# A conditional jump at the end of TensorE's and VectorE's programs, announced by a branch hint

## The chip, the cores and the metric

The kernel runs on one core of a Trainium2 chip. A core has five engines that each run a program of their own: TensorE (PE; its weight loads are listed apart as PEld), VectorE (DVE), ScalarE (ACT), GpSimd (POOL) and SyncE (SP). They meet through semaphores, and 16 DMA engines move data between the chip's memory and the core. The metric is the device time of one execution in microseconds (us), lower is better. It is compared as a median over runs; one execution is also recorded by the hardware profiler, and all views below are of that one.

## The reference, cut to what matters

One decode step: a layernorm, attention of one query token over the last 2048 positions of a key and value cache, and an MLP gate.

```
x  : 2 x 1 x 448            (B, S, D)     k_cache, v_cache : 2 x 8 x 8192 x 256
wq : 448 x 4096             wo : 4096 x 448       w1 : 448 x 1792      w2 : 1792 x 448

xn  = layernorm(x)
q   = (xn @ wq) as 16 heads of 256
s   = softmax(q k^T / 16) over the last 2048 positions; two query heads share one of 8 key heads
o   = (s v) put together to 2 x 4096, @ wo
g   = silu(relu(xn @ w1) @ w2)
out = x + o * g
```

All inputs and the output are bfloat16. Nearly all bytes are the two cache windows (16.8 MB each), the rest are the weights.

## The kernel before, in words

The kernel writes each engine's list of operations by hand. `_Prog` (line 23) holds five lists; `op` appends an operation, `dma` a transfer, each with the operations that it depends on. `run` (line 39) numbers the semaphores and then emits the lists one after the other: for every dependency that isn't known to be met it puts a wait (line 65) ahead of the operation. An engine works strictly in the order of its list. All of this is one straight block of code without a loop or a jump; an engine's program ends with its last operation.

The cache windows are taken as four units `u` (batch and half of the key heads) of 4 MB each, in four buffers `kv0` to `kv3`. SP issues all large loads in this order: wq, w1, w2, the four key units, then the value units into the same buffers as soon as the scores of that unit are done (`load_v`, the last unit in two halves), and last wo in six parts of 16, 4, 4, 4, 2 and 2 column tiles (`WO_PARTS`). Every one of these transfers is cut by rows over the 16 DMA engines, and its semaphore counts 16, one for each DMA engine, so that a part is there when the slowest of the 16 has brought its share.

The work goes in this order. VectorE and ScalarE do the layernorm and clear the banks. TensorE computes q (into `qbk`), then the MLP (`do_H`, `do_F`), VectorE makes the gate `g_sb`. For each key unit VectorE transposes the 4 MB buffer in four pieces (`do_turn`, line 276), TensorE makes the scores (`do_S`, into `sbk`), VectorE the maximum, ScalarE the exponentials (`do_max`), VectorE transposes them (`do_et`). `do_spread` puts all weights in place on TensorE, VectorE masks them (`do_pt`), then TensorE does the value products (`do_PV`, into `obk`) and VectorE scales them (`do_out`). At the end TensorE multiplies with wo, part by part as it lands (`direct`, into `fbk`; short unneeded products, `fill`, keep TensorE busy in between), and VectorE does the two last operations: the product with the gate (line 474) and the sum with x (line 476, `out_sb`). The output goes out in two halves, one issued by SP and one by ACT, and each of these two engines then waits for its own store:

```
        for c, eng in ((0, SP), (1, ACTE)):
            d_o = pr.dma(eng, out[:, 0, NCOL * c:NCOL * c + NCOL], out_sb[32 * c:32 * c + B, :], [v_o])
            pr.op(eng, None, [d_o])
```

TensorE, VectorE and GpSimd wait for no store.

Built, TensorE's program has 929 instructions of 64 bytes each, VectorE's 90, ScalarE's 27, SyncE's 24 and GpSimd's 20. An engine's instructions reach it by DMA too: the profile counts those packets as kind "instruction", on queues of their own.

Of the kernel before, what the change touches and what calls it, by code (L numbers as in the profile page):

```python
# [11 lines left out]
PE, DVE, ACTE, SP, POOL = "pe", "dve", "act", "sp", "pool"  # L12


class _Op:
    __slots__ = ("eng", "fn", "deps", "dma", "needed", "value", "sem")

    def __init__(self, eng, fn, deps, dma):
        self.eng, self.fn, self.deps, self.dma = eng, fn, deps, dma
        self.needed, self.value, self.sem = dma, 0, None  # L20


class _Prog:

    def __init__(self, nc, es):
        self.nc, self.es = nc, es
        self.lists = {PE: [], DVE: [], ACTE: [], SP: [], POOL: []}

    def op(self, eng, fn, deps=()):
# [9 lines left out]
    def run(self):  # L39
        nc = self.nc  # L40
        n = 0
        for ops in self.lists.values():
            for o in ops:
                for d in o.deps:
                    d.needed = True
        for e, ops in self.lists.items():
            sem, count = self.es.enter_context(nc.semaphore(f"s_{e}")), 0
            for o in ops:
                if o.dma:
                    n += 1  # L50
                    o.sem, o.value = self.es.enter_context(nc.semaphore(f"d_{n}")), 16
                elif o.needed:
                    count += 1
                    o.sem, o.value = sem, count

        def emit(eng, ops):
            seen = {}
            for o in ops:
                want = {}
                for d in o.deps:  # L60
                    if d.value > want.get(id(d.sem), (None, 0))[1]:
                        want[id(d.sem)] = (d.sem, d.value)
                for key, (sem, value) in want.items():
                    if value > seen.get(key, 0):
                        eng.wait_ge(sem, value)
                        seen[key] = value
                made = o.fn(eng) if o.fn else None
                if o.needed:
                    made.then_inc(o.sem, 16 if o.dma else 1)

        for eng, e in ((nc.sync, SP), (nc.gpsimd, POOL), (nc.scalar, ACTE), (nc.vector, DVE), (nc.tensor, PE)):
            emit(eng, self.lists[e])


def bass_recurrent_scan__sliding_block_cached__dense_activation_relu__decode_kernel(
# [11 lines left out]
    B, Sq, D = A_x.shape  # L87
# [14 lines left out]
    NCOL = D // 2  # L102
# [5 lines left out]
    with es:  # L108
        pr = _Prog(nc, es)

        def named(name, shape, dt):
            return es.enter_context(nc.sbuf_tensor(name, shape, dt))
# [4 lines left out]
        def view(t, off, dims, n=128, p0=0):  # L117
            width = t.shape[1]
            return bass.AP(t, p0 * width + off, [[width, n]] + dims)
# [28 lines left out]
        out_sb = named("out_sb", [128, NCOL], BF)  # L148
# [43 lines left out]
        for u in range(NU):  # L192
# [4 lines left out]
            out=ident[:, :], in_=ident[:, :], compare_op=ALU.not_equal, fill=1.0,  # L197
# [7 lines left out]
            out=sd[0:B, 0:1], in0=st2[0:B, 1:2], scalar1=EPS, scalar2=None, op0=ALU.add), [v_ag])  # L205
# [5 lines left out]
        def z(t):  # L211
            return a_z[t.name]
# [20 lines left out]
        for e2 in range(2):  # L233
            v_xn = pr.op(DVE, lambda e, e2=e2: e.tensor_scalar(  # L234
                out=view(xg, 128 - 127 * e2, [[256, 4], [128, 2], [2, 64]], n=B),
# [4 lines left out]
        def mm(out_ap, lhsT, rhs, start, stop=False, **kw):  # L240
            return lambda e: e.matmul(out_ap, lhsT=lhsT, rhs=rhs, start=start, stop=stop,  # L241
                                      skip_group_check=True, **kw)

        for s in range(SLOTS):
# [3 lines left out]
            out=view(xr, 0, [[4, SLOTS], [2, 2], [1, 2]]), in0=view(mbk, 0, [[2, SLOTS], [0, 2], [1, 2]]),  # L248
# [4 lines left out]
        for s in range(SLOTS):  # L253
# [6 lines left out]
            out=view(q_x, 0, [[256, 8], [128, 2], [1, 32]]), in0=view(qbk, 0, [[64, 8], [1, 2], [2, 32]]),  # L260
# [12 lines left out]
        def do_turn(u, lo, hi):  # L273
            kf = kv[u][:, :].bitcast(F32)
            for n in range(lo, hi):
                st["turn", u] = pr.op(DVE, lambda e, n=n: e.transpose(  # L276
                    kf[:, 2048 * n:2048 * n + 2048], kf[:, 2048 * n:2048 * n + 2048]), [d_k[u]])

        def do_S(u):
            b, hg = divmod(u, 2)  # L280
            deps = [st["turn", u], st["q"], z(sbk[u % 2]), st.get(("exp", u - 2))]
            for jp in range(8):
                j, par = divmod(jp, 2)
                for g in range(4):
                    o = pr.op(PE, mm(sbk[u % 2][32 * g:32 * g + 8, :],
                                     view(qstat, jp * 16 + 4 * g + 2 * hg + b, [[128, 8]]),
                                     view(kv[u], 64 * j + 2 * g + par, [[DH, NT], [8, 8]]),
                                     jp == 0, jp == 7, tile_position=(0, 32 * g)), deps)
                    deps = []
            last_S[u] = o  # L290
# [30 lines left out]
        def do_pt(u):  # L321
            st["pt", u] = pr.op(DVE, lambda e: e.tensor_tensor(  # L322
                out=view(pt[u], 0, [[8, 64], [2, 4], [1, 2]]), in0=view(spk, 128 * u, [[2, 64], [0, 4], [1, 2]]),
                in1=view(pmask, 0, [[0, 64], [1, 4], [0, 2]]), op=ALU.mult), [st["sp"], v_pm])
# [48 lines left out]
        def do_H():  # L373
            deps = [st["w1"], v_xr, v_q]
            for s in range(SLOTS):
                for k in range(4):
                    hf, i = divmod(k, 2)
                    lo = s * FC + i * 448
                    o = pr.op(PE, mm(qbk[32 * k:32 * k + B, 0:448], xr[:, 4 * s + 2 * hf:4 * s + 2 * hf + 2],
                                     w1_sb[:, lo:lo + 448], s == 0, s == SLOTS - 1, tile_position=(0, 32 * k)), deps)  # L380
                    deps = []
            v = pr.op(DVE, lambda e: e.tensor_scalar(
                out=h_n[:, :], in0=view(qbk, 0, [[1, 14], [14, 32]]),
                scalar1=0.0, scalar2=None, op0=ALU.max), [o])
            st["h"] = pr.op(DVE, lambda e: e.transpose(h_sb[:, :], h_n[:, :]), [v])

        def do_F():
            deps = [st["w2"], st["h"], z(fbk)]
            for j in range(14):
                i = j % 4  # L390
                o = pr.op(PE, mm(fbk[32 * i:32 * i + B, 0:D], h_sb[:, 32 * j:32 * j + 2], w2_sb[:, j * D:j * D + D],
                                 j < 4, j >= 10, tile_position=(0, 32 * i)), deps)
                deps = []
            v = pr.op(DVE, lambda e: e.tensor_copy(zc[:, :], fbk[:, 0:D]), [o])
            deps = [v, v_f8, st["mbk"]]
            for c in range(2):
                o = pr.op(PE, mm(mbk[32 * c:32 * c + B, 0:NCOL], f8[:, 0:B], zc[:, NCOL * c:NCOL * c + NCOL],
                                 True, True, tile_position=(0, 32 * c)), deps)
                deps = []
            a_e = pr.op(ACTE, lambda e: e.activation(ea[0:ROWS, :], mbk[0:ROWS, 0:NCOL], ACT.Exp, scale=-1.0), [o])  # L400
            v = pr.op(DVE, lambda e: e.tensor_scalar(
                out=ea[0:ROWS, :], in0=ea[0:ROWS, :], scalar1=1.0, scalar2=None, op0=ALU.add), [a_e])
            v = pr.op(DVE, lambda e: e.reciprocal(tmp[0:ROWS, :], ea[0:ROWS, :]), [v])
            st["g"] = st["mbk"] = pr.op(DVE, lambda e: e.tensor_tensor(
                out=g_sb[0:ROWS, :], in0=mbk[0:ROWS, 0:NCOL], in1=tmp[0:ROWS, :], op=ALU.mult), [v])
# [3 lines left out]

        do_H()  # L410
        do_F()
        do_turn(0, 0, 4)
        do_S(0)
        d_v[0] = load_v(0)
# [16 lines left out]
        do_rs()  # L431
        for u in range(1, NU):
            do_pt(u)
        for u in range(NU):
            do_PV(u)
            do_out(u)
            if u >= 2:
                do_turn_out(u - 2)
# [7 lines left out]
        for j in range(WO_TILED):  # L446
            i = j % 4
            o = pr.op(PE, mm(wbk[32 * i:32 * i + B, 0:D], at2[:, B * j:B * j + B], wqo[:, j * D:j * D + D],
                             j < 4, j >= WO_TILED - 4, tile_position=(0, 32 * i)), deps + [landed.get(j)])
# [19 lines left out]
        for j in range(20, 32):  # L469
# [5 lines left out]
            out=tmp[0:ROWS, :], in0=fbk[0:ROWS, 0:NCOL], in1=g_sb[0:ROWS, :], op=ALU.mult), [m_o, st["g"]])  # L475
        v_o = pr.op(DVE, lambda e: e.tensor_tensor(  # L476
            out=out_sb[0:ROWS, :], in0=tmp[0:ROWS, :], in1=x_c[0:ROWS, :], op=ALU.add), [v_t] + d_xc)
        for c, eng in ((0, SP), (1, ACTE)):
            d_o = pr.dma(eng, out[:, 0, NCOL * c:NCOL * c + NCOL], out_sb[32 * c:32 * c + B, :], [v_o])
            pr.op(eng, None, [d_o])  # L480

        pr.run()

# [27 lines left out]
```

## Time and profile before

| | |
|---|---|
| three runs | 110.45, 110.6 and 111.1 us; median 110.6 us |
| the profiled execution | 110.67 us |
| its span, from the first to the last instruction | 109.3 us |
| mean granted TensorE clock | 0.842 |
| busy: VectorE / TensorE / ScalarE / GpSimd | 62.2 / 57.0 / 9.1 / 2.1 us |
| DMA | 44.17 MB in 2616 packets, 404 GB/s over the span |
| last part of wo landed | 106.75 us |
| store issued; SP's wait for it over | 108.02 us; 109.3 us |

The span counts from the kernel's first instruction to its last. The time of the same execution is 1.32 us longer (110.67 less 109.35 in the trace's full figure); what lies in that difference isn't in the profile. The queue named q1 is SP's ring of data transfers, q10 ACT's; q8 and q14 are queues that carry instructions.

### The profile page before, as it was taken

The page shows a single profiled execution, that of the slowest core. Times are in us where ns is not written, and L with a number is a line of the kernel's source. Part 1 is how long each engine was busy: PE and PEld are TensorE (multiplying, and loading weights), DVE is VectorE, ACT ScalarE, POOL GpSimd, SP SyncE. Part 2 cuts the span into 40 slices and gives each one's busy share as a digit, 9 for nine tenths or more (in the row PEclk, how much of TensorE's full clock was granted, in tenths as well). Part 3 has the DMA queues.
Part 4 walks back from the last instruction along what each step waited for, and adds up shares of the span by engine and source line. Part 5 has one row for each costly group of instructions (what it writes and reads, how often), then busy time and mean ns, then how long its engine had stood idle before and what let it go on. Part 6 is the DMA issues. An engine that isn't in the chain of part 4 may idle for free.

```text
span 109.3 us, 1081 instructions
## 1 busy us (share of the span) xinstructions
PE 57.0 (52%) x458; PEld 14.5 (13%) x458; DVE 62.2 (57%) x83; ACT 9.1 (8%) x18; POOL 2.1 (2%) x12
## 2 busy tenths in 40 slices
PE   0010559430000079929952994499339555937791
PEld 0000114100000011001100120010023122413230
DVE  2920046445099979999999999930457333004102
ACT  3970000010000000002000200020110000000000
POOL 7000000000000000000000000000000000000000
PEclk9999999985555555999995569958995999999999
DMA  6899999999999999999999999999999899999940
GB/s 168 336 452 397 408 436 501 396 455 438 444 396 455 467 408 396 455 467 408 408 458 444 408 420 467 432 420 402 467 432 420 378 444 420 444 413 410 405 187 1
DMA packets 2616, 44.17 MB, mean 404 GB/s; under 512 B 306, under 2 KB 564, under 8 KB 948
## 3 DMA queue, kind: packets, MB, share of 16 engines
q1 hardware_dynamic: 2596, 44.11, 94.7%
q8 instruction: 3, 0.05, 0.2%
q14 instruction: 1, 0.01, 0.0%
q10 hardware_dynamic: 16, 0.00, 0.0%
HBM read 44.11 MB, written 0.00 MB: 403 GB/s over the span
## 4 chain that ended last, share of the span: by engine, by line
DMA 57%; DVE 28%; PE 7%; SPq 5%; issue 1%
DMA kv<-in_A_k_cache_dram 34%; DVE kv L276 24%; DMA wqo<-in_A_wo_dram 23%; PE sbk L241 7%; SPq L35 5%; DVE q_x L305 1%; DVE rm L293 1%; DVE rm_t L295 0%; DVE bias L299 0%; DVE bt L296 0%; DVE tmp L474 0%; DVE out_sb L476 0%; PE fbk L241 0%
## 5 line engine op out<-in xcount | busy, mean ns | idle before, releaser
L241 PE MATMUL sbk<-kv,qstat 128*8 128x512 bf16 x128 | 29.9, 1086 | 23.9 <-DVE kv L276 23.9
L276 DVE STREAM_TRANSPOSE kv<-kv 128x2048 f32<-128x2048 f32 x16 | 35.6, 2276 | 4.6 <-DMA kv<-in_A_k_cache_dram 4.6
L241 PE MATMUL obk<-kv,pt 128*16 128x512 bf16 x128 | 9.3, 435 | 4.8 <-DVE xg L356 2.4
L241 PEld LDWEIGHTS sbk<-kv,qstat 128*8 128x8 bf16 x128 | 4.0, 107 | 48.4 <-DVE kv L276 30.2
L353 DVE TENSOR_SCALAR o_odd<-obk,rs 128x256 f32<-128x256 f32 x4 | 1.9, 484 | 11.6 <-PE obk L241 11.6
L300 ACT ACTIVATE e_sb<-sbk,bias 128x512 bf16<-128x512 f32 x4 | 2.7, 687 | 52.6 <-DVE bias L299 52.6
L241 PE MATMUL qbk<-wqo,xr 128*4 128x512 bf16 x28 | 3.2, 626 | 5.7 <-DMA wqo<-in_A_wq_dram 5.7
L259 DVE TENSOR_SCALAR q_x<-qbk 128x512 bf16<-128x512 f32 x1 | 0.7, 691 | 8.7 <-PE qbk L241 8.7
L293 DVE TENSOR_REDUCE rm<-sbk 128x1 f32<-128x512 f32 x4 | 2.6, 662 | 4.7 <-PE sbk L241 4.7
L241 PE MATMUL sbk<-kv,ident 128*32 128x512 bf16 x19 | 5.1, 380 | 0.0
L241 PEld LDWEIGHTS obk<-kv,pt 128*16 128x16 bf16 x128 | 3.2, 97 | 10.1 <-issue 5.8
L305 DVE STREAM_TRANSPOSE q_x<-e_sb 128x512 bf16<-128x512 bf16 x4 | 2.8, 691 | 1.7 <-ACT e_sb L300 1.7
L241 PE MATMUL mbk<-ident,xg 2*128 2x2 bf16 x7 | 0.3, 163 | 6.0 <-DVE xg L234 6.0
L322 DVE TENSOR_TENSOR pt<-spk,pmask 128x512 bf16<-128x512 f32 x4 | 2.6, 684 | 0.7 <-PE spk L241 0.7
L241 PE MATMUL qbk<-w_sb,xr 128*2 128x448 bf16 x28 | 2.8, 572 | 0.0
L241 PE MATMUL fbk<-wqo,at 128*2 128x224 bf16 x32 | 2.5, 258 | 0.4 <-DMA wqo<-in_A_wo_dram 0.4
L241 PE MATMUL spk<-q_x,perm 128*32 128x128 bf16 x16 | 0.6, 292 | 3.1 <-DVE q_x L305 3.1
L474 DVE TENSOR_TENSOR tmp<-fbk,g_sb 34x224 f32<-34x224 f32 x1 | 0.4, 383 | 3.1 <-PE fbk L241 3.1
L270 DVE CAST qstat<-mbk 32x256 bf16<-32x256 f32 x4 | 1.7, 421 | 0.7 <-PE mbk L241 0.7
L356 DVE SCALAR_TENSOR_TENSOR xg<-obk,rs,o_odd 128x256 bf16<-128x256 f32 x4 | 1.9, 484 | 0.1
L451 DVE COPY wc<-wbk 128x448 f32<-128x448 f32 x1 | 0.6, 625 | 2.4 <-PE wbk L241 2.4
L241 PEld LDWEIGHTS sbk<-kv,ident 128*32 128x32 bf16 x19 | 1.8, 97 | 1.8
(70 smaller groups left out, 33.1 us busy)
## 6 DMA issues: line engine op xcount, KB each, us to landing
kv<-in_A_k_cache_dram SPq DMA_DIRECT2D x4, 4096.0 KB, 41.3
kv<-in_A_v_cache_dram SPq DMA_DIRECT2D x3, 4096.0 KB, 22.1
kv<-in_A_v_cache_dram SPq DMA_DIRECT2D x2, 2048.0 KB, 18.0
wqo<-in_A_wq_dram SPq DMA_DIRECT2D x1, 3584.0 KB, 11.3
w_sb<-in_B_w_dram SPq DMA_DIRECT2D x2, 1568.0 KB, 16.2
wqo<-in_A_wo_dram SPq DMA_DIRECT2D x1, 1792.0 KB, 23.7
wqo<-in_A_wo_dram SPq DMA_DIRECT2D x3, 448.0 KB, 24.8
wqo<-in_A_wo_dram SPq DMA_DIRECT2D x2, 224.0 KB, 25.5
```

Of the source, the lines that this page charges most:

```text
L35: o = _Op(eng, lambda e: e.dma_start(dst, src), [d for d in deps if d is not None], True)
L241: return lambda e: e.matmul(out_ap, lhsT=lhsT, rhs=rhs, start=start, stop=stop, skip_group_check=True, **kw)
L259: v_q = pr.op(DVE, lambda e: e.tensor_scalar(out=view(q_x, 0, [[256, 8], [128, 2], [1, 32]]), in0=view(qbk, 0, [[64, 8], [1, 2], [2, 32]]) ...
L270: st["q"] = st["mbk"] = pr.op(DVE, lambda e, Q=Q: e.tensor_copy(qstat[32 * Q:32 * Q + 32, 256 * Q:256 * Q + 256], mbk[32 * Q:32 * Q + 32, ...
L276: st["turn", u] = pr.op(DVE, lambda e, n=n: e.transpose(kf[:, 2048 * n:2048 * n + 2048], kf[:, 2048 * n:2048 * n + 2048]), [d_k[u]])
L293: v = pr.op(DVE, lambda e: e.tensor_reduce(out=rm[:, 0:1], in_=sbk[u % 2][:, :], axis=AX.X, op=ALU.max), [last_S[u], p_z, st.get(("rmt", u ...
L300: st["exp", u] = pr.op(ACTE, lambda e: e.activation(e_sb[:, :], sbk[u % 2][:, :], ACT.Exp, bias=bias[:, 0:1], accum_out=ssum[:, u:u + 1]), ...
L305: st["et", u] = pr.op(DVE, lambda e: e.transpose(q_x[:, 512 * u:512 * u + 512], e_sb[:, :]), [st["exp", u], m_qt])
L322: st["pt", u] = pr.op(DVE, lambda e: e.tensor_tensor(out=view(pt[u], 0, [[8, 64], [2, 4], [1, 2]]), in0=view(spk, 128 * u, [[2, 64], [0, 4 ...
L353: v = pr.op(DVE, lambda e: e.tensor_scalar(out=o_odd[:, :], in0=obk[:, DH:2 * DH], scalar1=rs[:, 2 * u + 1:2 * u + 2], scalar2=None, op0=A ...
L356: st["osb", u] = pr.op(DVE, lambda e: e.scalar_tensor_tensor(out=o_sb[:, lo:lo + DH], in0=obk[:, 0:DH], scalar=rs[:, 2 * u:2 * u + 1], in1 ...
L451: v_wc = pr.op(DVE, lambda e: e.tensor_copy(wc[:, :], wbk[:, 0:D]), [o])
```

## The change: what it does

Three things are added; no operation on data is changed, moved or removed.

1. At one place in VectorE's list (ahead of the first `do_turn`) and one in TensorE's (ahead of the first `do_PV`) a register is set to zero and a branch hint is emitted. The hint names the jump that stands at the end of that engine's program.
2. At the end of their lists TensorE and VectorE wait for both stores. Then they compare the register with zero and jump: if equal (it always is) to `fin`, otherwise to `over`, a block of a no-operation and a jump to `fin`. `fin` is empty; what follows there is the end of the engine's program.
3. SyncE, GpSimd and ScalarE get an unconditional jump to `fin`, without a hint. On SyncE and ScalarE this stands behind their wait for the store, as before.

TensorE's program grows from 929 to 935 instructions, VectorE's from 90 to 96, and the other three by two each. In the list of TensorE the hint follows the last matmul of `do_spread`; in VectorE's it follows the operation that makes `g_sb`.

```
@@ class _Prog
+        self.tell = {}
         self.lists = {PE: [], DVE: [], ACTE: [], SP: [], POOL: []}
@@ _Prog.run
+        ends = {PE: nc.tensor, DVE: nc.vector}
+        zero, told = {}, {}
+
+        def announce(e):
+            def fn(eng):
+                zero[e] = eng.alloc_register(f"zero_{e}")
+                eng.reg_mov(zero[e], 0)
+                told[e] = eng.mark_branch_hint_location()
+            return fn
+
+        for e in ends:
+            o = _Op(e, announce(e), [], False)
+            self.lists[e].insert(self.tell[e], o)
         for eng, e in ((nc.sync, SP), (nc.gpsimd, POOL), (nc.scalar, ACTE), (nc.vector, DVE), (nc.tensor, PE)):
             emit(eng, self.lists[e])
+        for e, eng in ends.items():
+            eng.br_eq(zero[e], 0, "fin", "over").branch_hint(told[e])
+        nc.br("fin", engines=[eng.engine for eng in (nc.sync, nc.gpsimd, nc.scalar)])
+        with nc.body("over", valid_engines=[eng.engine for eng in ends.values()]):
+            for eng in ends.values():
+                eng.nop()
+                eng.br("fin")
+        nc.switch_bb("fin")
@@ the kernel
         do_H()
         do_F()
+        pr.tell[DVE] = len(pr.lists[DVE])
         do_turn(0, 0, 4)
...
             do_pt(u)
+        pr.tell[PE] = len(pr.lists[PE])
         for u in range(NU):
             do_PV(u)
...
+        stores = []
         for c, eng in ((0, SP), (1, ACTE)):
-            d_o = pr.dma(eng, out[:, 0, NCOL * c:NCOL * c + NCOL], out_sb[32 * c:32 * c + B, :], [v_o])
-            pr.op(eng, None, [d_o])
+            stores.append(pr.dma(eng, out[:, 0, NCOL * c:NCOL * c + NCOL], out_sb[32 * c:32 * c + B, :], [v_o]))
+            pr.op(eng, None, stores[-1:])
+        for eng in (PE, DVE):
+            pr.op(eng, None, stores)
```

## The prediction

> **What bounds the kernel now.** I read the chain that ended last first, then the DMA queues, then windows over the last microseconds. From 81.24 us on, the chain in order of time is one DMA and what hangs on it:
>
> ```profile
> 81.24 25.50 DMA wqo<-in_A_wo_dram
> 106.75 0.04 issue
> 106.79 0.38 PE fbk L241 x4
> 107.17 0.02 issue
> 107.19 0.40 DVE tmp L474
> 107.58 0.02 issue
> 107.61 0.38 DVE out_sb L476
> ```
>
> The columns are start, duration and what ran. The last part of wo lands at 106.75 us; four matmuls, two VectorE operations and the store follow, 2.6 us up to the end at 109.35. The page's DMA row (busy tenths in 40 slices) is full from the second slice to the 37th, so the loads are one unbroken queue. What sets 106.75 is when the slowest of the 16 DMA engines has worked off its share. The queue table shows who else uses those engines:
>
> ```profile
> q1 hardware_dynamic: 2596, 44.11, 94.7%
> q8 instruction: 3, 0.05, 0.2%
> q14 instruction: 1, 0.01, 0.0%
> ```
>
> Three packets of 16 KB and one of 8 KB carry instructions. The trace keeps each packet's start, duration and size, and packets of one DMA engine stand end to end (the next starts 4 ns before the last one ends), so each can be put to its engine. The four fetches, and the data packet right behind each on the same engine:
>
> ```
> fetch, us    queue, size    took       next data packet      normal for its size   delay of that engine
> 25.77        q8, 16 KB      962 ns     32 KB, 1681 ns        1213 ns               1.42 us
> 54.78        q14, 8 KB      309 ns     32 KB, 1744 ns        1213 ns               0.84 us
> 74.54        q8, 16 KB      960 ns     32 KB, 1681 ns        1213 ns               1.42 us
> 96.17        q8, 16 KB      947 ns     14 KB, 1005 ns        535 ns                1.41 us
> ```
>
> The delay is the time from the fetch's start to that of the next data packet (948, 306, 946 and 943 ns), plus what that packet takes over the normal. A delayed engine never catches up, since each has a fixed share. Windows over the end show it (the last two columns are the busy share of the 16 DMA engines, and GB/s):
>
> ```profile
> 105.40:105.50 0.10, 0.10 (x1) 0.00 (x0) 0.00 (x0) 0.00 (x0) 0.00 (x0) 1.00 0.28 108
> 105.60:105.80 0.20, 0.09 (x2) 0.09 (x4) 0.00 (x0) 0.00 (x0) 0.00 (x0) 1.00 0.21 81
> 106.15:106.25 0.10, 0.10 (x6) 0.02 (x4) 0.00 (x0) 0.00 (x0) 0.00 (x0) 1.00 0.09 36
> 106.30:106.40 0.10, 0.10 (x4) 0.02 (x4) 0.00 (x0) 0.00 (x0) 0.00 (x0) 1.00 0.05 18
> ```
>
> A packet's records overlap a little, so shares run slightly high. 13 engines are through by 105.50 us. Then three work (0.21 x 16 = 3.4), then two, then one. Strung from packet to packet, the three are those of the 16 KB fetches: the engine of 25.77 us ends its data at 106.11, that of 96.17 at 106.27 and that of 74.54 at 106.48. Call them A, D and C. The engine of the 8 KB fetch, B, is already among the thirteen. So the instruction fetches cost this execution 106.48 - 105.50 = 0.98 us, and C alone decides.
>
> **The change, part by part.**
>
> *The hints.* TensorE's fetches fall where some 194, 450 and 706 of its instructions have gone, 256 apart (256 x 64 bytes is the 16 KB packet): each time it enters a block it fetches the next. TensorE's hint is its 487th or so instruction, inside the block entered shortly before 74.5 us; its target is instruction 935, in the block entered near 93.4 us, the one already fetched. If a hint directs the next fetch, the one at 96.17 (D) has nothing to bring and goes. VectorE's hint is its 33rd instruction, ahead of its crossing near the 48th that made the fetch at 54.78, so B goes likewise. The fetches of A and C bring blocks that the kernel needs and lie ahead of TensorE's hint. Gain: D's end falls by 1.41 us to 104.86, B's by 0.84, and the landing stays at 106.75 because C doesn't move. **Zero in this execution.** Were C not there, D's removal would be worth 106.27 - 106.11 = 0.16 us against A.
>
> *Cost of issuing the hints.* A register move and a hint on each. The nearest rows are the sequencer's own waits:
>
> ```profile
> L65 PEldq EVENT_SEMAPHORE  x9: 51/51/4100, 1.7 to 102.4; - x9
> L65 DVEq EVENT_SEMAPHORE  x3: 21/21/50, 3.8 to 107.2; - x3
> L65 ACTq EVENT_SEMAPHORE  x1: 17/17/17, 109.2 to 109.2; - x1
> L65 SPq EVENT_SEMAPHORE  x1: 17/17/17, 109.3 to 109.3; - x1
> ```
>
> (minimum, median, maximum in ns; the 4100 is a wait). Two such are 0.04 to 0.1 us. VectorE's lie in its idle 3.79 us ahead of the first transpose, which waits for the key load; TensorE's in the 0.57 us in which it waits for VectorE's `pt` ahead of the first value product. Nothing is late. Without that cover 0.1 us would still vanish into the wo load that ends last.
>
> *The waits for the stores.* Behind them on TensorE and VectorE stands only the jump, and nobody waits for those engines inside the kernel. The later of the two stores is seen at 109.33 (SP's row), 1.3 us after its issue at 108.02, and SP already waits for it.
>
> *The jumps.* These come after 109.33 on the path that sets the end. No row shows a branch. From below a sequencer instruction of 17 ns (SP's wait), from above the longest sequencer step at this end, 0.33 us for the issue of the store at 108.02. I take 0.1 us: two of TensorE's 51 ns steps, wait and compare, being nearest in kind. The Trainium skill ("Advanced Engine Details and Errata", Control Flow Timing) gives about 108 ns for compare-and-branch and 51 ns for a plain one; the sum by it would be the same within 0.01 us.
>
> *Sum.* Profiled execution: 110.67 - 0 + 0.1 = 110.8 us. The median of the three runs lies 0.07 below the profiled one, so against that median **110.7 us**, no difference that counts (1% is about what a measurement of this kernel can tell from no change). Its own range is 110.3 to 111.2.
>
> **The rivals.**
>
> *Another engine is last in most executions (0.20).* Which DMA engine gets which fetch need not be the same each time, and the three runs differ by 0.65 us. Before any fetch the 16 engines stand within 0.88 us of each other (end of the first key unit, 27.95 to 28.83 us on engines without a fetch). If D falls on a late engine and A and C on early ones, removing D gains up to 0.88; if D shares an engine with A or C, 1.41. For: the spread of the runs. Against: here D is 0.2 us behind C. Typical gain 0.4 us: 110.3; at the end of the scale 109.2. Of the 0.20, 0.05 lie more than 1% below before.
>
> The page "Runtime: NRT & Kernel Launch" of the Trainium skill (Instruction fetch mechanics) holds that crossing a 16 KB block is one bump of a DMA tail, mostly hidden. By that rule removing fetches gains nothing anywhere; the trace disagrees on the cost (1.41 us of one DMA engine each) though not on my sum.
>
> *The end gets longer: slower (0.24).* The code behind the kernel's last instruction has to be there as well. Before, the block after the last one is fetched at 96.17 us, well ahead. If that fetch is suppressed, TensorE has 962 - 935 = 27 instructions left in its block and must then fetch one with nothing to cover it: latency of a small transfer as the store shows it, 1.3 us, and 0.95 us for the 16 KB, together 2.2. VectorE (blocks of 8 KB, 128 instructions, crossing at 48) has 80 left and is better covered. The time is 1.32 us longer than the span, so something outside the span is counted. It decides if that something reaches past those 27 instructions: 110.7 + 2.2 = 112.9, or 111.9 upward if half of it is covered. For: before, no instruction packet follows 96.17, so the end found its code in place. Against: 1.32 us may well lie ahead of the first instruction, and 27 instructions at 51 ns take 1.4 us, which hides much of a fetch that starts at the jump.
>
> The same page of the Trainium skill (Instruction fetch mechanics, and the breakdown under The launch sequence) says that a taken branch out of the current window waits for its target's block, and counts the barriers and resets behind a kernel in microseconds; here the target itself is inside the block, and no run so far shows what follows it.
>
> *The change doesn't do what it says (0.08).* The hint fetches its target at once, or the crossing fetches anyway. The packet of 96.17 then stays, or stands near 82 us, one engine is 1.41 us late as before, and C still ends last: 110.8. Only if it hits C's engine does the load land 1.4 us later: 112.1 (0.02 of the 0.08).
>
> **How the numbers follow.** Forecast 0.48, another engine last 0.20, longer end 0.24, no effect 0.08. Faster by over 1%: 0.06, which is 0.05 of the first rival and 0.01 taken from the forecast for what I can't see. Slower by over 1%: 0.24 + 0.02 = 0.26. Within 1%: the remaining 0.68. Range 109.9 to 112.3: it takes in the forecast and most of the first rival, and the covered half of the longer end; what is left out are the far gains (0.05) and the full 2.2 us (0.12).
>
> **What would show it.** Right: no instruction packet near 96.17 and 54.78; two DMA engines, no longer three, working after 105.6; wo landing still at 106.75; the last rows of the span are branches near 109.4. Wrong: a landing of wo below 106.5 (another engine decided); an instruction packet after 109.3 together with a time that stands more than 1.5 us above its span (the end is longer); a packet still at 96 or one near 82 (the hint does nothing, or fetches itself).

## The result, and the profile after

The median of 20 runs of the changed kernel is 111.16 us, that of 20 runs of the kernel before, taken beside them, 110.59 us. Two of the 20, at 112.41 and 112.45 us, lie over 1.5% above the fastest one and are left out of the ratio and of the counts below; their spans are ordinary (109.4 us), so 3.0 us lie beyond them, and the median of the other 18 is 111.12. The ratio is 1.0048 (95% interval 1.0025 to 1.0072): slower by half a per cent, inside the range that was predicted and inside "within 1%", but clear of zero.

The profiled execution took 112.03 us, and its span is 109.39 us. So 2.64 us lie beyond the span, where the profiled execution of before had 1.32. The chain ends as it did before (start, duration, what ran):

```profile
81.55 25.01 DMA wqo<-in_A_wo_dram
106.56 0.04 issue
106.60 0.37 PE fbk L264 x4
106.98 0.03 issue
107.00 0.39 DVE tmp L499
107.39 0.02 issue
107.42 0.38 DVE out_sb L501
```

The last part of wo lands at 106.56 us, where it was 106.75. The queue table of the page has lost one packet of q8, and the row of q14 is gone:

```profile
q1 hardware_dynamic: 2596, 44.11, 94.8%
q8 instruction: 2, 0.03, 0.1%
q10 hardware_dynamic: 16, 0.00, 0.0%
```

The two packets of q8 start at 24.71 and 74.28 us. Those of before at 96.17 (16 KB) and 54.78 us (8 KB) don't come. Windows over the end of the wo load (last columns: share of the 16 DMA engines, GB/s):

```profile
105.60:105.80 0.20, 0.20 (x8) 0.17 (x4) 0.00 (x0) 0.00 (x0) 0.00 (x0) 1.00 0.14 54
106.00:106.10 0.10, 0.10 (x4) 0.06 (x4) 0.00 (x0) 0.00 (x0) 0.00 (x0) 1.00 0.14 54
106.15:106.25 0.10, 0.10 (x4) 0.00 (x0) 0.00 (x0) 0.00 (x0) 0.00 (x0) 1.00 0.05 18
```

Two DMA engines work after 105.6 us (0.14 x 16 = 2.2) instead of three. In number that fits the two 16 KB fetches that stayed; the trace doesn't name a packet's engine. What is new stands at the end. The rows of the added jumps (minimum, median and maximum in ns, then the first and last start in us; DVEq and PEldq are the conditional ones, ACTq and SPq the unconditional ones, and GpSimd's has no row):

```profile
L89 DVEq COMPARE_BRANCH  x1: 78/78/78, 109.2 to 109.2; - x1
L89 PEldq COMPARE_BRANCH  x1: 235/235/235, 109.2 to 109.2; - x1
L90 ACTq COMPARE_BRANCH  x1: 33/33/33, 109.0 to 109.0; - x1
L90 SPq COMPARE_BRANCH  x1: 33/33/33, 109.1 to 109.1; - x1
```

SP sees its store and starts its jump at 109.144. Before, its 17 ns wait was the end of the span. Now TensorE's jump starts at 109.157, takes 235 ns and ends the span at 109.392. And the DMA queues from 109.4 to 113 us hold one packet:

```profile
DMA packets 1, 0.02 MB, mean 5 GB/s; under 512 B 0, under 2 KB 0, under 8 KB 0
## 3 DMA queue, kind: packets, MB, share of 16 engines
q8 instruction: 1, 0.02, 2.3%
```

It starts at 110.926, 1.53 us after the end of TensorE's jump, and takes 1341 ns. It is a 16 KB packet on the queue that lacks its fetch at 96 us, so it is read below as that fetch, put off.

### The profile page after: what moved, and what is told of

It reads as the page before. It is cut to its first block, busy times and chain, and to the rows that moved or that the text cites. A ratio compares the mean times of both kernels' runs of the same rounds, so it can differ in the third digit from the quotient of the medians.

```text
span 109.4 us, 1089 instructions
## 1 busy us (share of the span) xinstructions
PE 57.0 (52%) x458; PEld 14.8 (14%) x458; DVE 62.2 (57%) x83; ACT 9.1 (8%) x18; POOL 2.1 (2%) x12
## 4 chain that ended last, share of the span: by engine, by line
DMA 57%; DVE 28%; PE 7%; SPq 5%; issue 1%
DMA kv<-in_A_k_cache_dram 34%; DVE kv L299 24%; DMA wqo<-in_A_wo_dram 23%; PE sbk L264 7%; SPq L36 5%; DVE q_x L328 1%; DVE rm L316 1%; DVE rm_t L318 0%; DVE bias L322 0%; DVE bt L319 0%; DVE tmp L499 0%; DVE out_sb L501 0%; PE fbk L264 0%
## 5 line engine op out<-in xcount | busy, mean ns | idle before, releaser
L264 PE MATMUL obk<-kv,pt 128*16 128x512 bf16 x128 | 8.8, 415 | 4.6 <-DVE xg L379 2.4
```

## The experiments

Each run has a time and a span. The difference, the time beyond the span, is far steadier than either, and so it is listed too. Spans are recorded to 0.1 us, so a single difference is good to 0.05. The 76 runs of the kernel before that were taken beside the experiments are put together in the first row; each ratio is to those taken beside that kernel. The last three columns of "after" hold 18 runs.

```
kernel            median us  ratio to before (95%)      span, mean us   beyond the span: median, min to max   runs above 1.7
before             110.65    -                          109.37          1.33   1.27 to 1.38                    0 of 76
after              111.16    1.0048 (1.0025..1.0072)    109.47          1.60   1.52 to 2.63                    6 of 18
e1_no_hint         111.14    1.0055 (1.0035..1.0075)    109.60          1.62   1.55 to 1.66                    0 of 6
e2_no_wait         110.84    1.0019 (1.0004..1.0034)    109.29          1.43   1.37 to 2.21                    2 of 12
e3_wait_only       110.96    1.0035 (1.0021..1.0048)    109.40          1.56   1.56 to 1.64                    0 of 6
e4_pe_only         111.33    1.0079 (1.0051..1.0107)    109.53          1.82   1.53 to 2.84                    4 of 7
e5_dve_only        110.83    1.0020 (0.9998..1.0041)    109.38          1.55   1.48 to 1.57                    0 of 12
e6_pad64           111.48    1.0078 (1.0044..1.0112)    109.76          1.73   1.57 to 2.50                    5 of 8
e7_pe_wait         111.08    1.0032 (1.0009..1.0056)    109.47          1.58   1.54 to 1.62                    0 of 12
e8_jump_only       111.02    1.0025 (1.0002..1.0047)    109.56          1.41   1.36 to 1.49                    0 of 12
e9_sp_waits        110.59    0.9998 (0.9982..1.0014)    109.35          1.33   1.28 to 1.37                    0 of 12
e10_act_waits      110.78    1.0007 (0.9994..1.0020)    109.32          1.46   1.42 to 1.54                    0 of 12
e11_pad8           111.15    1.0048 (1.0031..1.0065)    109.48          1.73   1.54 to 1.86                    6 of 9
e12_less20         111.35    1.0059 (1.0036..1.0082)    109.71          1.57   1.54 to 2.07                    2 of 7
```

A span's mean is known to some 0.05 us for before (109.37), and to 0.1 to 0.2 us for the others.

**1. Without the hints.**

```
-                told[e] = eng.mark_branch_hint_location()
...
-            eng.br_eq(zero[e], 0, "fin", "over").branch_hint(told[e])
+            eng.br_eq(zero[e], 0, "fin", "over")
```

> The two hints are left out; the jumps and TensorE's and VectorE's waits for the stores stay. Theory T (a fetch put off: the hint takes the fetch at 96 us away, and it is made up after the jump, at 110.93 us in the changed kernel's profile, where the time still counts): the fetches at about 54.8 and 96.2 us are back, none follows the jump, and the time is before plus the jump, 110.7 to 110.8 us. Rival J (the jumps and the later arrival of TensorE and VectorE at what follows cost the 0.57 us themselves): 111.1 to 111.2 us, as in the changed kernel.

All four fetches are back (25.98, 54.72, 74.20, 97.18 us), no packet follows the jump, and the time is still 111.14, as J had it. Theory T falls as the main cause: the put-off fetch isn't what the median pays for. What went with the hints is the slow tail: beyond the span no run is above 1.66 us, where the changed kernel has 6 of 18 above 1.7. Six runs alone would not show that, but all the runs together do: with TensorE's hint (after, 2, 4, 6, 11, 12) 25 of 61 are above 1.7, without it (1, 3, 5, 7 to 10) none of 72. TensorE's jump takes 209 ns without a hint, and the mean span is 0.23 us above before (known to about 0.2):

```profile
L88 DVEq COMPARE_BRANCH  x1: 63/63/63, 109.2 to 109.2; - x1
L88 PEldq COMPARE_BRANCH  x1: 209/209/209, 109.2 to 109.2; - x1
```

**2. Without the waits for the stores.**

```
-        for eng in (PE, DVE):
-            pr.op(eng, None, stores)
```

> Hints and jumps stay; TensorE and VectorE don't wait for the stores and jump when their last operation is done, near 107.2 and 108.0 us. T: no fetch at 96 us; TensorE's packet starts some 1.5 us after its jump, near 108.7, and is over by about 109.7, so that nothing or little is left of the loss: 110.5 to 110.8 us. J: TensorE and VectorE are early again and the jumps of SyncE and ScalarE cost some 0.03 us: 110.6 as well. Neither would give 111.1; that would say that the hint does harm elsewhere.

110.84: above both theories' 110.5 to 110.8 by little. TensorE's jump stands at 106.54, the fetch follows at 108.06, beside the stores:

```profile
q8 instruction: 1, 0.02, 2.0%
q10 hardware_dynamic: 4, 0.00, 0.1%
q1 hardware_dynamic: 4, 0.00, 0.1%
```

(DMA queues from 107 to 110 us; q10 and q1 are the two stores.) The jumps have left the span, whose mean of 109.29 is the lowest of all, and 1.43 instead of 1.60 us lie beyond it. So the waits cost about a sixth of a microsecond there, even with the hints.

**3. The waits alone.** The jumps, the hints and the blocks `over` and `fin` are taken out; what stays against before is:

```
+        for eng in (PE, DVE):
+            pr.op(eng, None, stores)
```

> No hints and no jumps on any engine; TensorE and VectorE wait for both stores as in the changed kernel. T: the four fetches as before, 110.6 us. J, if the late arrival of the two engines costs: 110.9 to 111.1 us.

110.96, and 1.56 us beyond the span in six runs that differ by 0.08. The span is unchanged (109.40 against 109.37). J holds for the waits: they cost 0.23 us, all of it after the last instruction that the profile shows. The rows of the waits bear this out. TensorE's and VectorE's last ones start near 108.96 us and end with SP's at 109.15, so nothing in the span is later for them:

```profile
L66 PEldq EVENT_SEMAPHORE  x10: 51/51/3091, 1.7 to 109.0; - x10
L66 DVEq EVENT_SEMAPHORE  x4: 21/36/186, 4.0 to 109.0; - x4
L66 ACTq EVENT_SEMAPHORE  x1: 17/17/17, 109.0 to 109.0; - x1
L66 SPq EVENT_SEMAPHORE  x1: 17/17/17, 109.1 to 109.1; - x1
```

**4. TensorE alone.**

```
-        ends = {PE: nc.tensor, DVE: nc.vector}
+        ends = {PE: nc.tensor}
...
-        nc.br("fin", engines=[eng.engine for eng in (nc.sync, nc.gpsimd, nc.scalar)])
+        nc.br("fin", engines=[eng.engine for eng in (nc.sync, nc.gpsimd, nc.scalar, nc.vector)])
...
-        for eng in (PE, DVE):
+        for eng in (PE,):
```

> Hint, wait and conditional jump on TensorE alone; VectorE ends as before, but for a jump without a hint. T: the fetch near 54.8 us is back, the one at 96 us stays away and follows the jump; the whole loss remains, 111.0 to 111.2 us, because TensorE has 27 instructions of its block left and VectorE 80. Rival: VectorE's put-off fetch is what costs; then 110.7 us here.

111.33: the whole loss and the tail are there (4 of 7 above 1.7 us), with VectorE's fetch back at 54.71. The tail is TensorE's. The time is above the 111.0 to 111.2 expected. That the tail's cause is the number of instructions left was not shown by this run; 6, 11 and 12 try it.

**5. VectorE alone.** The mirror image of 4: `ends` holds VectorE only, TensorE jumps without hint or wait.

> Hint, wait for the stores and conditional jump on VectorE alone; TensorE ends as before but for a jump without a hint and without a wait. Theory W (what costs is TensorE: its late arrival adds 0.25 us to what is counted beyond the span, its conditional jump 0.2 us to the span, the put-off fetch of its block a tail on some runs): time less span stays near 1.32 to 1.40 us, no run above 1.5, the fetch at 54.8 us is gone, that at 96 us is there: 110.6 to 110.75 us. Rival V (either engine's late arrival costs the same): time less span 1.55 us, 110.9 us.

1.55 us beyond the span, not 1.32 to 1.40. W falls and V holds: VectorE's late arrival costs about as much as TensorE's (jumps on other engines are in this figure too; no run has VectorE's wait without them). The span is as before and there is no tail, as W had it: VectorE's jump takes 78 ns, and no 8 KB fetch shows in the trace behind it.

**6. TensorE's end moved past the block boundary.** Behind `do_F`, where TensorE idles:

```
+        for _ in range(32):
+            pr.op(PE, mm(sbk[0][0:32, 0:32], ident[:, 0:32], ident[:, 0:32], True, True), [z(sbk[0]), p_id])
```

> The changed kernel with 32 unneeded small matmuls (64 instructions) on TensorE near 23 us, where it idles up to 39 us; they write a bank that the scores then overwrite. They shift the end of TensorE's program past the next block boundary, so that some 200 instructions of its last block lie behind it instead of 30 or fewer. W with the put-off fetch as the cause of the slow tail: time less span 1.55 to 1.65 us in every run, the tail above 1.8 us gone, median 111.0 to 111.1 us; a 16 KB fetch near 96 us is back, since that block is now needed. Rival (the tail comes from the hint or the jump as such, not from missing code): the tail stays, about one run in three above 1.8 us beyond its span.

The block is fetched again, at 93.67 us, as expected. But 5 of 8 runs are above 1.7 us, two of them above the 1.8 that the expectation named (1.81 and 2.50). With some 200 instructions left behind the end TensorE should not run out of code there, unless more than that follow the kernel, which no run shows. So this speaks against a wait for missing code. It doesn't speak against a put-off fetch as such: TensorE enters its last block near 105.5 us (about the 962nd of its instructions in the trace starts at 105.55), and no fetch of the block behind that one is in the trace either. The mean span is 0.34 us above that of the runs of before taken beside it (109.42), known to 0.2; the jump explains 0.23.

**7. TensorE's wait alone.** Before, with one line more: `pr.op(PE, None, stores)`.

> The kernel before, with nothing but TensorE's wait for both stores added at its end. W: time less span 1.55 us, 110.9 us, as where both engines wait. Rival V2 (VectorE's wait is what costs): 1.32 us beyond the span, 110.6 us.

1.58 us beyond the span. Together with 3 and 5: TensorE late, VectorE late, or both, it is 1.55 to 1.58. The cost doesn't add up over engines. The median, 111.08, is above the 110.9 expected; what lies beyond the span is as W had it.

**8. The jumps alone.** Edits 1 and 2 together: no hints, no waits.

> The jumps on all five engines, without hints and without the waits of TensorE and VectorE. W: TensorE's 0.24 us jump lies at 106.6 us, 2.5 us ahead of the end, and costs nothing; span as before, time less span 1.35 to 1.42 us, no slow tail: 110.65 to 110.7 us. Rival: if jumps cost by themselves, 110.85 us as with hints and no waits.

1.41 us beyond the span and no tail, as W had it. That is 0.08 us more than before, so the jumps by themselves cost a little there. The total is 111.02, above both expectations; the spans are longer too, 109.56 against 109.42 for the runs of before taken beside it, with TensorE's and VectorE's jumps at 106.76 and 107.58 us, where nothing waits for them. The longer span is known to 0.15 us only, so that part isn't settled.

**9 and 10. Who waits last.** The kernel before, with both stores waited for by one engine, SP in 9 and ACT in 10:

```
-            pr.op(eng, None, [d_o])
+        pr.op(SP, None, stores)
```

> The kernel before, with one edit: SyncE waits for both stores and ScalarE, which still issues its own, waits for none. Theory L (what lies beyond the span grows with which engines arrive last: 1.33 us with SyncE and ScalarE, 1.57 as soon as TensorE or VectorE or both arrive late): with SyncE alone it is 1.33 us or less, down to 1.1 if ScalarE counts as the other two do; 110.4 to 110.6 us. Rival (what matters is only that some engine waits till the end): 1.33 us and no change.

> The kernel before, with ScalarE waiting for both stores and SyncE, which still issues its own, for none. L: between 1.1 and 1.57 us beyond the span, and different from SyncE alone if the engines differ in what follows their last instruction; 110.4 to 110.9 us. Rival: 1.33 us, no change.

SP alone gives 1.33 us, the same as SP and ACT; ACT alone 1.46. So the order is SP 1.33, ACT 1.46, TensorE or VectorE 1.55 to 1.58. L holds: what counts is which engines arrive last, and SP is the cheapest, as the kernel before already has it. Neither run beats the kernel before.

**11 and 12. TensorE's end 8 instructions nearer to its block's end, and 20 farther.** In 11 the loop of 6 with four products; in 12:

```
-                    fill(10)
```

> The changed kernel with four unneeded small matmuls (8 instructions) on TensorE in its idle time near 23 us; the scores then overwrite what they write. TensorE's program ends 8 instructions nearer to its block's end. If the slow tail comes from waiting for the put-off block, more runs have it and its size grows: more than half above 1.8 us beyond the span, median 111.4 us or more. Rival (the tail doesn't hang on the place of the end): 1.57 us in most runs, about one in three above 1.7, median 111.1 to 111.2.

> The changed kernel without the ten products in the last value unit whose results nothing uses (20 instructions), so that TensorE's program ends 20 instructions farther from its block's end. If the slow tail comes from waiting for the put-off block, it is gone or rare: no more than one run in eight above 1.7 us beyond the span, median 110.95 to 111.1 us, if TensorE's lower load doesn't slow the end by its clock. Rival: the tail stays as in the changed kernel, one run in three.

With 8 more instructions 6 of 9 runs are above 1.7 us, with 20 fewer 2 of 7, with 64 more 5 of 8, and 6 of 18 as it stands. Above 1.8, the bound that the expectation for 11 named, they are 1 of 9, 2 of 7, 2 of 8 and 5 of 18. The size doesn't grow either (1.86 at most in 11), and the median of 11, 111.15, is the rival's. These are few runs, but they show no trend with the place of the end, so the theory of missing code finds no support here. In 12 the median (111.35) is above both expectations because the span is longer (109.71 us). Its trace shows a second effect of the edit: from 98 to 101 and from 101 to 104 us the granted clock is 0.50 and 0.57, where the changed kernel's has 1.00 in both, and the chain that ends last runs through TensorE's products instead of the load of wo.

What the tail is, two profiled executions tell in part. In 12 the profiled one is in the tail (111.67 us, 2.05 beyond its span), and the window from 109.6 to 113 us again has one packet:

```profile
DMA packets 1, 0.02 MB, mean 5 GB/s; under 512 B 0, under 2 KB 0, under 8 KB 0
## 3 DMA queue, kind: packets, MB, share of 16 engines
q8 instruction: 1, 0.02, 2.3%
```

```
                     packet of q8, us        its end less the first MEMSET (0.236, 0.235)     time of that execution
after                110.926 to 112.267      112.031                                           112.03
12 (20 fewer)        110.671 to 111.909      111.674                                           111.67
```

The first MEMSET on GpSimd is the first busy instruction of the program. In both executions the time, which is given to 0.01 us, equals the stretch from there to the end of the put-off packet. So in these two the time ends with the packet. Profiles with a smaller excess (1.84 us in 4, 1.72 in 6, 1.57 in 11) hold no packet behind the jump. What makes those of 4 and 6, and the two tail runs of 2, in whose profile the packet lies early, stays open. Shown is that the tail comes with TensorE's hint; how, beyond these two executions, is not.

## Why the prediction was right, and where it was not

The time was forecast at 110.7 us, within 1%, range 109.9 to 112.3. It came out at 111.16, 0.57 us above the kernel before, where the sum had 0.1. That it stayed within 1% is in part luck: the terms that the sum left out or had too small happened to be small. One sign that the prediction named for being wrong did appear, an instruction packet after 109.3 us with a time more than 1.5 us above its span. By its steps:

- **The hints take two fetches away: right.** No packet at 54.78 and 96.17 us; three late DMA engines become two. Every kernel with the hint on the engine in question shows it, and every one without has the fetch back. In 6 a fetch near 94 us brings the block that holds the jump, which is needed, and no fetch of the one behind it is seen. The prediction's instruction counts at the fetches, 194, 450 and 706, are 199, 445 and 756 by the rows of the trace that had started; the third fetch comes some 2.8 us after the 706th, and the conclusion stands.
- **The removed fetches are worth nothing, because C ends last: right within what can be told.** With the two 16 KB fetches that lie ahead of the hint, two late engines are left, and they decide. The nine profiled executions that have the fetch between 93 and 100 us land their last wo part at 106.33 to 106.86, 106.61 on average; the five without it at 106.45 to 106.58, 106.51. That is 0.1 us in favour of the change, less than the scatter. It would fit the rival that another engine is sometimes last, at a quarter of that rival's typical gain of 0.4 us. The changed kernel's own profile, at 106.56, lies between the 106.75 that the prediction named as its sign and the 106.5 that would have spoken against it.
- **Issuing the hints costs nothing: not contradicted.** The hint itself took 45 ns on TensorE at 80.9 us and 51 ns on VectorE at 26.1 us, on the sequencers, while the engines still worked on what had been put in ahead. The next work on each had something else to wait for: TensorE's first value product, at 82.29 us, for VectorE, and VectorE's first transpose, at 30.23, for the key load.
- **"Nobody waits for those engines inside the kernel", so the waits cost nothing: wrong.** Inside the kernel it holds, and the span stays (109.40 against 109.37 with the waits alone). But the time doesn't end there. What is counted beyond the span is 1.33 us when SP is last and 1.56 when TensorE or VectorE is as late: +0.23 us, a term that the sum put at nothing. The prediction had seen the 1.32 us beyond the span, but asked only whether a missing block would lengthen them.
- **The jumps cost 0.1 us: the mechanism right, the size wrong.** TensorE's takes 0.235 us and ends the span; from the moment at which SP sees its store, the span lasts 0.248 us where it lasted 0.017, +0.23 us. It lies inside the bounds given (0.02 to 0.33), well above the row that was held for nearest. Beyond the span the jumps add 0.05 to 0.08 us more (1.61 in 1 against 1.56 in 3 and, without waits, 1.41 in 8 against 1.33). The Trainium skill ("Advanced Engine Details and Errata", Control Flow Timing) gives about 108 ns for a compare-and-branch and 51 ns for a plain branch. Neither agrees with these traces: the conditional jump takes 209 to 242 ns on TensorE and 63 to 78 on VectorE, the unconditional one 32 to 33 on SP and ACT.
- **The rival "the end gets longer": happened, only in part for the reason given.** The put-off packet does come after the jump, something outside the span does count, and in two profiled executions the time ends with that packet. But the 0.23 us that every run pays come from late arrival, with or without a hint. The tail, up to 1.1 us over the 1.56 in a third of the 18 runs, comes with TensorE's hint and doesn't depend on the 27 instructions left in the block, as far as 6, 11 and 12 can tell. (The rival's 111.9 for a half-covered fetch starts from 110.8; from its own 110.7 it is 111.8.) The page "Runtime: NRT & Kernel Launch" of the Trainium skill (Instruction fetch mechanics) has a taken branch out of the current window wait for its target's page. No jump of these runs leaves its block, by the instruction counts, so none of them tests that.

A sum that fits, made afterwards: 110.59 + 0.23 (late arrival) + 0.05 (the jumps, beyond the span) + 0.23 (TensorE's jump) - 0.1 (earlier landing, within the scatter) = 111.0, and the tail, which is 0.15 us on average over 18 runs (the mean beyond the span is 1.76 there, less the 1.61 of the same kernel without hints): 111.15, against a median of 111.12 for these 18. Several terms are known to 0.05 or 0.1 us only, so the close fit proves nothing by itself.

## What to carry to other kernels

Before an engine that had finished is made to wait for the end, ask what is counted after its last instruction: here the engine that finishes last sets 1.33 (SP), 1.46 (ACT) or 1.56 us (TensorE, VectorE) that no row of the profile shows, and a conditional jump on TensorE costs 0.2 us where it ends the span. Look at a run's time and its span apart: in the kernel before the difference was steady to 0.05 us, which is all that the recorded spans resolve, where each of the two scattered by 0.9 to 1, and it separated causes that the totals could not. A transfer taken off one DMA engine gained next to nothing here, because others still ended last. And a fetch that a hint takes away can come back at the end, where nothing covers it.

## What the runs showed of the hardware that was not expected

- In the profile of the kernel before, an instruction fetch of 16 KB sets one of the 16 DMA engines back by 1.41 to 1.42 us, though the packet takes only 0.95 us: the next data packet on that engine takes 0.47 us longer than normal. An 8 KB fetch costs 0.84 us. The lag stays to the end of the load: after 105.6 us three DMA engines still work with three such fetches, two with two.
- A branch hint ahead of the crossing takes the next block's fetch away (none at 54.78 us with VectorE's hint, none at 96 with TensorE's). In three profiles a packet makes it up 1.05 to 1.53 us after the end of TensorE's jump (runs 12, 2 and the changed kernel); in those of 4 and 11 none is seen. The window shows no other packet at that time in 12 and in the changed kernel, and yet it took 1.24 and 1.34 us there, against 0.92 to 0.97 amid the full load.
- A jump is not the same on all engines: 32 to 33 ns on SP and ACT (unconditional), 63 on VectorE and 209 on TensorE (conditional), and 78 and 235 to 242 there with a hint.
